# Linear attention and a mixture of adapters on one core: batch 0 loaded in another way, transposes copied in pairs, and a new written-out order

## The chip, the cores and the metric

The kernel runs on one core of a Trainium2 chip. Five engines work side by side, each with its own instruction queue: TensorE (PE in the profile) multiplies matrices and transposes, VectorE (DVE) and ScalarE (ACT) do elementwise work and copy results out of PSUM, GpSimd (POOL) issues the loads, and SyncE (SP) issues the stores. The metric is the device time of one execution in microseconds.

## The reference, cut to what matters

There are 8 batches of 8 heads, 576 positions and 64 features per head, all in float32. Queries and keys go through a relu and are then doubled: once multiplied by the cosine and once by the sine of an angle that grows with the position. The attention is linear, so it is two matrix products and a division:

```
phi(x)  = [relu(x) * cos, relu(x) * sin]       # 128 features
kv      = phi(k)^T v         z = sum over positions of phi(k)
x       = (phi(q) kv) / (phi(q) . z + 1e-6)
```

The heads of a position are put side by side: x has 4608 rows of 512. For every row `logits = x @ w_gate` picks the two largest of 8 experts and weights w from a softmax over the two. The output is `x + sum over the two of w * (x @ A[e]) @ B[e]`, with A of 512x16 and B of 16x512 for each expert.

## The kernel before, in words

**Tiling.** The 4608 rows are worked through in 36 groups of 128 rows. A group is either "one" (two sets of 64 rows of the same batch, position slots x and x+4) or "two" (slot j of two neighbouring batches). The batches form four pairs; the first three pairs have eight groups "one" and one "two" (slot 8), the last pair has nine groups "two". Three groups form a set for the adapters; the last two sets have two groups and one. Sets 0 to 6 cover the first 21 groups.

**Stages of a batch.** K is loaded and gets a relu; V is loaded and multiplied by the cosine and the sine (`vscale`, one call for each); `kv_mm` forms the products K'V in PSUM, and `kv_evac` copies them to the tile BD. Loads by POOL's queue convert float32 to bfloat16 on the way. For batch 0, K and V are loaded by SP's queue as float32 into buffers that later hold outputs (`load_early`). Batches 0 and 1 are loaded in two halves of four heads.

**Stages of a group.** `qt_mm` transposes Q in eight pieces, `qt_evac` copies it to SBUF with a relu (cosine half; the cosine itself cancels in the division), `qt_tan` multiplies by the tangent (the second half), `num_mm` forms numerator and denominator, `x_rden` and `x_xt` divide. `xt_mm` and `xt_evac` transpose x for the adapters.

**Stages of a set.** `za_mm` multiplies by A and the gate weights; eight small steps pick the experts and their weights; `zg_mm` transposes the weighted result; `dx_mm` adds x (a product with the identity) and the adapter's output in PSUM; `osb` copies 128x512 float32 to an output buffer, and `store` writes it. Groups of equal kind and batch that follow each other are stored together. A group "two" is stored from 128 partitions; a group "one" is stored by two transfers, each from 64 partitions, since its halves go to different rows.

**What sets the order.** All steps are entered in a plan with `pl.add` (engine, duration in microseconds, a due time, what it needs, makes and occupies). They are not scheduled at run time: `ORDER` is the sequence in which they are issued, `CHOICE` picks ScalarE or VectorE where a step has both, `SLOTS` gives the buffer of each use. Each engine therefore works through its own steps in the sequence of `ORDER` and waits in place for what a step needs. `HOLD` makes a store wait until a given load has landed. The durations are those that a search used when it wrote the lists; nothing reads them when the kernel is built.

**Buffers.** PSUM has two tiles of two banks (`pND`, for K'V and numerators) and four of one bank (`pS`, for everything else). There are 7 output buffers of three groups each, so a set from 7 on takes the buffer of an earlier set when all stores of that set have landed.

**Stores before.** SP's sequence begins with both halves of set 0, then parts of sets 2, 1, 1, 1, 3, 4 and 4. Three stores are held by loads: the second by V of batch 4, the fourth by K of batch 5, the thirteenth by Q of batch 7.

**Warm-up.** `pe_warm` issues 26 products of a constant tile into an unused bank before any data is there.

Of the kernel before, what the change touches and what calls it, by code (L numbers as in the profile page):

```python
# [9 lines left out]
FP32 = mybir.dt.float32  # L10
# [10 lines left out]
    24, 13, 25, 3, 18, 30, 14, 19, 31, 0, 1, 15, 5, 32, 16, 4, 22, 2, 6, 17, 7, 21, 26, 8, 11, 9, 40, 12, 10, 28, 46,  # L21
    47, 41, 33, 20, 27, 29, 42, 34, 48, 35, 118, 56, 134, 119, 36, 135, 110, 120, 37, 57, 111, 43, 136, 126, 39, 38,
    127, 58, 112, 121, 49, 128, 113, 122, 50, 65, 114, 51, 115, 44, 66, 129, 116, 123, 45, 130, 67, 23, 124, 53, 131,
    117, 74, 132, 125, 137, 138, 133, 52, 139, 75, 142, 55, 54, 398, 143, 150, 399, 140, 151, 144, 166, 400, 403, 145,
    141, 401, 152, 167, 174, 59, 76, 153, 175, 168, 158, 402, 154, 159, 404, 146, 405, 160, 406, 147, 407, 155, 61,
    83, 408, 161, 60, 410, 412, 162, 148, 411, 169, 149, 156, 84, 163, 182, 413, 183, 62, 157, 409, 184, 170, 414,
    176, 164, 171, 64, 190, 416, 191, 85, 68, 63, 177, 192, 165, 185, 178, 417, 172, 186, 421, 418, 179, 419, 187,
    420, 180, 422, 173, 188, 423, 102, 193, 189, 69, 206, 181, 424, 198, 207, 436, 194, 70, 199, 425, 222, 94, 195,
    426, 223, 214, 437, 71, 427, 224, 441, 215, 438, 200, 439, 216, 440, 442, 208, 201, 92, 77, 72, 196, 73, 430, 443,
    428, 197, 431, 209, 202, 203, 429, 444, 230, 210, 445, 204, 231, 217, 79, 101, 78, 446, 450, 415, 447, 448, 205,  # L30
    238, 218, 211, 455, 93, 219, 225, 456, 232, 239, 460, 80, 226, 457, 451, 458, 227, 459, 449, 461, 246, 240, 233,
    81, 462, 452, 254, 247, 234, 463, 262, 235, 82, 103, 434, 278, 263, 248, 241, 86, 279, 249, 433, 255, 464, 212,
    242, 250, 469, 256, 213, 467, 243, 432, 470, 465, 251, 468, 257, 264, 466, 220, 258, 228, 280, 221, 236, 471, 259,
    281, 229, 87, 244, 237, 473, 245, 252, 260, 282, 474, 265, 253, 261, 475, 478, 493, 266, 476, 267, 477, 270, 494,
    268, 271, 479, 498, 480, 269, 310, 272, 481, 311, 495, 88, 273, 482, 286, 318, 287, 487, 274, 496, 275, 497, 483,
    488, 288, 89, 484, 499, 283, 319, 489, 105, 276, 91, 302, 294, 90, 106, 295, 289, 277, 485, 303, 290, 512, 296,
    486, 291, 297, 492, 513, 284, 304, 292, 298, 285, 517, 305, 514, 299, 293, 515, 306, 300, 320, 516, 307, 301, 321,
    518, 312, 530, 322, 500, 308, 519, 501, 309, 313, 531, 502, 95, 520, 521, 505, 532, 104, 526, 506, 533, 522, 314,
    535, 534, 315, 527, 524, 536, 523, 323, 107, 525, 537, 529, 97, 538, 108, 507, 316, 539, 324, 317, 508, 542, 325,
    544, 96, 511, 109, 550, 545, 334, 551, 98, 335, 543, 336, 548, 326, 552, 100, 99, 342, 540, 327, 528, 553, 555,  # L40
    337, 554, 541, 328, 503, 556, 338, 343, 557, 547, 329, 504, 344, 546, 558, 374, 330, 559, 350, 331, 509, 358, 351,
    564, 339, 510, 345, 359, 352, 454, 565, 332, 360, 549, 353, 346, 375, 347, 568, 340, 333, 366, 491, 354, 341, 361,
    367, 355, 348, 562, 368, 349, 362, 356, 376, 369, 563, 363, 357, 569, 453, 370, 371, 364, 382, 570, 365, 372, 377,
    571, 383, 373, 572, 490, 574, 586, 573, 384, 575, 435, 378, 390, 576, 560, 472, 391, 587, 577, 379, 385, 578, 591,
    588, 561, 380, 392, 579, 386, 381, 589, 567, 387, 393, 590, 580, 566, 592, 388, 394, 593, 581, 389, 583, 395, 582,
    594, 603, 584, 595, 396, 604, 596, 585, 397, 605, 608, 598, 606, 607, 600, 597, 609, 610, 599, 622, 601, 611, 632,
    612, 623, 617, 602, 624, 627, 618, 625, 613, 626, 614, 619, 628, 620, 629, 616, 615, 630, 631, 621, 633, 635, 634,
    636,
]
CHOICE = [  # L50
    0, 0, 0, 0, 0, 0, 0, 0, 0, 0, 0, 0, 0, 0, 0, 0, 0, 0, 0, 0, 0, 0, 0, 0, 0, 0, 0, 1, 1, 1, 0, 0, 0, 0, 0, 0, 0, 0,
    1, 0, 0, 0, 0, 0, 0, 1, 0, 0, 0, 1, 1, 0, 0, 0, 0, 1, 0, 0, 0, 0, 0, 1, 0, 0, 0, 0, 0, 0, 0, 0, 0, 0, 0, 0, 0, 0,
    0, 0, 1, 0, 0, 0, 0, 0, 0, 0, 0, 0, 0, 0, 0, 0, 0, 0, 0, 0, 0, 0, 0, 0, 1, 0, 0, 0, 0, 0, 0, 0, 0, 0, 0, 0, 0, 0,
    0, 0, 0, 1, 0, 0, 0, 0, 0, 0, 0, 1, 0, 0, 0, 0, 0, 0, 0, 0, 0, 0, 0, 0, 0, 0, 0, 0, 0, 0, 0, 0, 0, 0, 0, 1, 0, 0,
    0, 0, 0, 0, 0, 1, 0, 0, 0, 0, 0, 0, 0, 1, 0, 0, 0, 0, 0, 0, 0, 0, 0, 0, 0, 0, 0, 0, 0, 0, 0, 0, 0, 0, 0, 0, 0, 0,
    0, 0, 0, 0, 0, 0, 0, 1, 0, 0, 0, 0, 0, 0, 0, 1, 0, 0, 0, 0, 0, 0, 0, 0, 0, 0, 0, 0, 0, 0, 0, 0, 0, 0, 0, 0, 0, 0,
    0, 0, 0, 0, 0, 0, 0, 0, 0, 0, 0, 0, 0, 0, 0, 0, 0, 0, 0, 0, 0, 0, 0, 0, 0, 1, 0, 0, 0, 0, 0, 0, 0, 0, 0, 0, 0, 0,
    0, 0, 0, 0, 0, 0, 0, 0, 0, 0, 0, 0, 0, 0, 0, 0, 0, 0, 0, 0, 0, 0, 0, 0, 0, 0, 0, 0, 0, 0, 0, 0, 0, 0, 0, 0, 0, 0,
    0, 0, 0, 0, 0, 0, 0, 0, 0, 0, 0, 0, 0, 0, 0, 0, 0, 0, 0, 0, 0, 0, 0, 0, 0, 0, 0, 0, 0, 0, 0, 0, 0, 0, 0, 0, 0, 1,
    0, 0, 0, 0, 0, 0, 0, 0, 0, 0, 0, 0, 0, 0, 0, 0, 0, 0, 0, 0, 0, 0, 0, 0, 0, 0, 0, 0, 0, 0, 0, 1, 0, 0, 0, 0, 0, 0,  # L60
    0, 0, 0, 0, 0, 0, 0, 0, 0, 0, 0, 0, 0, 0, 0, 0, 0, 0, 0, 0, 0, 0, 0, 0, 0, 0, 0, 0, 0, 0, 0, 1, 0, 1, 0, 0, 0, 0,
    0, 0, 0, 0, 0, 0, 0, 0, 0, 0, 0, 0, 0, 0, 0, 0, 0, 0, 0, 0, 0, 0, 0, 0, 0, 0, 0, 1, 0, 1, 0, 0, 0, 0, 0, 0, 0, 0,
    0, 0, 0, 0, 0, 0, 0, 0, 1, 0, 0, 0, 0, 0, 0, 0, 0, 0, 0, 0, 0, 0, 0, 0, 0, 0, 0, 0, 0, 0, 0, 0, 0, 0, 0, 0, 0, 0,
    0, 0, 0, 0, 0, 0, 0, 0, 0, 0, 0, 0, 0, 0, 1, 0, 0, 0, 0, 0, 0, 0, 0, 0, 0, 0, 0, 0, 0, 0, 0, 0, 0, 0, 0, 0, 0, 0,
    0, 0, 0, 0, 0, 0, 0, 0, 0, 0, 0, 1, 0, 0, 0, 0, 0, 0, 0, 0, 0, 0, 0, 0, 0, 0, 0, 0, 0, 0, 0, 0, 0, 0, 0, 0, 0, 0,
    0, 0, 0, 0, 0, 0, 0, 0, 0, 0, 0, 0, 0, 0, 0, 0, 0, 0, 0, 0, 0, 0, 0, 0, 0, 1, 0, 0, 0, 0, 0, 1, 0, 0, 0, 0, 0, 0,
    0, 0, 0, 0, 0, 0, 0, 0, 0, 0, 0, 0, 1, 0, 0, 0, 0, 0, 0, 0, 0, 0, 0, 0, 0, 0, 0, 0, 0,
]
SLOTS = [
    0, 0, 1, 0, 1, 0, 2, 3, 0, 0, 0, 0, 1, 1, 1, 1, 2, 1, 2, 2, 0, 2, 3, 2, 3, 0, 0, 3, 1, 3, 4, 1, 1, 0, 0, 0, 0, 2,  # L70
    1, 1, 2, 2, 1, 1, 1, 3, 3, 1, 2, 0, 0, 2, 3, 2, 0, 1, 0, 1, 0, 1, 0, 1, 0, 1, 2, 1, 0, 3, 0, 2, 2, 3, 2, 2, 1, 0,
    1, 3, 3, 3, 0, 4, 0, 2, 4, 0, 4, 2, 5, 1, 0, 5, 3, 5, 3, 0, 0, 1, 6, 1, 0, 0, 6, 1, 2, 7, 2, 1, 2, 7, 1, 0, 8, 0,
# [9 lines left out]
]  # L82

HOLD = [
    (415, 75), (434, 83), (528, 103),
]


# [677 lines left out]
```

## Time and profile before

| | |
|---|---|
| time, median of 3 runs | 114.4 us (112.69 to 114.42) |
| profiled execution: its time | 111.68 us |
| profiled execution: its span | 109.6 us |
| granted TensorE clock | 0.98 of full |
| busy: TensorE, VectorE, ScalarE | 91.0, 94.3, 86.1 us |
| DMA moved | 25.29 MB; HBM read 28.85 MB, written 9.44 MB |

The span runs from the first instruction to the last, and the execution's time has 2.1 us around it. The times in the views are those of that one execution, from the span's start. A line such as `77.55 1.25 PE L417 MATMUL pnd<-VV,Kb ... x72` has start, duration, engine, line, operation, result and operands, form, and how many follow each other. [...] `q0` are the loads of POOL's queue, `q1` the transfers of SP's queue; each has packets, MB, and the time of its packets as a share of 16 DMA engines, which can exceed 100% since packets overlap. The line numbers are those of the kernel before.

### The profile page before, as it was taken

What the parts mean: (1) busy time and instruction counts of PE and PEld (TensorE: products, weight loads), DVE (VectorE), ACT (ScalarE), POOL (GpSimd) and SP (SyncE); (2) the same over time, 40 slices, a digit from 0 to 9 for tenths busy, and PEclk for the clock granted to TensorE, in tenths of its full rate; (3) what the DMA queues carried; (4) which work ended last, traced back from release to release, by engine and by line L of the source; (5) the groups of instructions that cost most, each with busy time, mean ns of one, the idle gap of its engine ahead of it and who ended that gap; (6) DMA issues with size and microseconds to landing.
All of it is one profiled execution on the core that took longest, in us unless ns stands there. A gap on an engine that the chain in (4) does not pass through costs nothing.

```text
span 109.6 us, 4027 instructions
## 1 busy us (share of the span) xinstructions
PE 91.0 (83%) x1670; PEld 65.2 (59%) x1670; DVE 94.3 (86%) x269; ACT 86.1 (78%) x192; POOL 22.8 (21%) x39
## 2 busy tenths in 40 slices
PE   2995296398787959989999989899998999999820
PEld 1342285277556846866878976776676678766200
DVE  5996765986999999999999999999996999887720
ACT  7889558996799639889999699867895987498730
POOL 7981754452222112222200000000000000000000
PEclk9999859999999999999999999999999999999998
DMA  2999999999999999999999999999994999998892
GB/s 76 393 305 269 207 206 193 203 207 210 206 210 209 205 278 209 207 209 277 207 209 307 240 277 207 218 217 256 179 254 103 220 234 285 280 197 226 343 377 109
DMA packets 17041, 25.29 MB, mean 231 GB/s; under 512 B 2176, under 2 KB 13568, under 8 KB 17024
## 3 DMA queue, kind: packets, MB, share of 16 engines
q0 software_dynamic: 13008, 13.25, 72.2%
q1 hardware_dynamic: 4016, 11.80, 34.3%
q8 instruction: 13, 0.21, 0.7%
q14 instruction: 4, 0.03, 0.1%
HBM read 28.85 MB, written 9.44 MB: 349 GB/s over the span
## 4 chain that ended last, share of the span: by engine, by line
DVE 44%; PE 28%; DMA 12%; ACT 6%; issue 4%; POOL 2%; SPq 0%; DVEq 0%; POOLq 0%; ACTq 0%
DVE xt L536 13%; DVE VV L406 10%; DMA Qb<-in_q_dram 8%; PE pnd L520 7%; PE pnd L417 6%; DVE qTcs L507 5%; PE ps L490 5%; DMA out_dram<-osb 4%; PE ps L544 3%; PE ps L557 3%; DVE zg L606 3%; ACT qTcs L495 2%; DVE osb L243 2%; DVE rden L531 2%; DVE BD L431 2%
## 5 line engine op out<-in xcount | busy, mean ns | idle before, releaser
L520 PE MATMUL pnd<-BD,qTcs 128*128 128x130 bf16 (+1 forms) x384 | 23.1, 223 | 3.4 <-DVE xt L536 1.5
L495 ACT ACTIVATE qTcs<-ps 128x512 bf16<-128x512 bf16 x36 | 20.9, 597 | 5.4 <-PE ps L490 4.8
L536 DVE TENSOR_TENSOR xt<-pnd,rden 128x512 bf16<-128x512 f32 x36 | 24.2, 683 | 0.2
L520 PEld LDWEIGHTS <-qTcs 128*128 128x128 bf16 (+1 forms) x384 | 18.2, 103 | 7.3 <-issue 5.1
L241 ACT COPY xT<-ps 128x512 bf16<-128x512 bf16 x26 | 14.6, 588 | 4.2 <-PE ps L544 3.9
L241 ACT COPY osb<-ps 128x512 f32<-128x512 f32 (+1 forms) x31 | 16.4, 558 | 1.4 <-DVE osb L243 1.3
L490 PE MATMUL ps<-ident,Qb 128*64 128x128 bf16 x288 | 14.2, 231 | 3.9 <-DMA Qb<-in_q_dram 3.2
L507 DVE TENSOR_TENSOR qTcs<-qTcs,TT 128x512 bf16<-128x512 bf16 x36 | 14.7, 410 | 2.0 <-ACT qTcs L495 1.6
L544 PE MATMUL ps<-ident,xt 128*128 128x128 bf16 x144 | 13.5, 222 | 2.6 <-DVE xt L536 2.2
L406 DVE TENSOR_TENSOR VV<-Vb,TV 128x2304 bf16<-128x2304 bf16 (+1 forms) x12 | 14.8, 1241 | 0.0
L628 PE MATMUL ps<-Ball,zgT 128*128 128x512 bf16 x36 | 13.7, 380 | 1.0 <-ACT zgT L241 1.0
L490 PEld LDWEIGHTS <-Qb 128*64 128x64 bf16 x288 | 9.7, 114 | 7.7 <-DMA Qb<-in_q_dram 3.7
L626 PE MATMUL ps<-xt,ident 128*128 128x512 bf16 x36 | 13.6, 380 | 0.0
L544 PEld LDWEIGHTS <-xt 128*128 128x128 bf16 x144 | 9.7, 115 | 5.3 <-DVE xt L536 3.2
L404 ACT ACTIVATE VV<-Vb,TVf 128x128 bf16<-128x128 bf16 (+1 forms) x36 | 12.7, 444 | 0.0
L417 PE MATMUL pnd<-VV,Kb 64*64 64x130 bf16 x576 | 11.1, 228 | 0.4 <-DVE xt L536 0.4
L417 PEld LDWEIGHTS <-Kb 64*64 64x64 bf16 x576 | 9.6, 112 | 2.3 <-issue 1.2
L557 PE MATMUL ps<-AW,xT 128*128 128x136 bf16 x144 | 10.7, 223 | 0.1
L429 ACT CAST BD<-pnd 64x520 bf16<-64x520 f32 x13 | 7.8, 597 | 3.6 <-DVE BD L431 2.2
L557 PEld LDWEIGHTS <-xT 128*128 128x128 bf16 x144 | 8.8, 98 | 1.7 <-issue 0.6
L292 PE MATMUL ps<-warm 128*128 128x512 bf16 x26 | 7.8, 474 | 2.0 <-DVE warm L286 2.0
L531 DVE RECIPROCAL rden<-pnd 128x8 f32<-128x8 f32 x36 | 7.2, 200 | 1.0 <-PE pnd L520 0.9
(57 smaller groups left out, 108.1 us busy)
## 6 DMA issues: line engine op xcount, KB each, us to landing
out_dram<-osb SPq DMA_DIRECT2D x16, 256.0 KB, 4.0
Kb<-in_k_dram POOLq DMA_DIRECT2D x6, 576.0 KB, 23.2
Vb<-in_v_dram POOLq DMA_DIRECT2D x6, 576.0 KB, 24.1
Qb<-in_q_dram POOLq DMA_DIRECT2D x6, 576.0 KB, 25.1
out_dram<-osb SPq DMA_DIRECT2D x6, 384.0 KB, 5.3
out_dram<-osb SPq DMA_DIRECT2D x2, 768.0 KB, 3.3
osb<-in_k_dram SPq DMA_DIRECT2D x2, 576.0 KB, 5.6
osb<-in_v_dram SPq DMA_DIRECT2D x2, 576.0 KB, 7.0
```

The lines of the kernel that those rows point to most:

```text
L241: nc.scalar.copy(o, i)
L406: nc.vector.tensor_tensor(out=o, in0=i, in1=TV[:, cs].unsqueeze(1).to_broadcast([128, n, J, D]), op=ALU.mult)
L417: nc.tensor.matmul(out=pt[64 * hh:64 * hh + 64, par, a * 2 * W:(a + 1) * 2 * W], lhsT=kt[r, 2 * a + hh, j, :], rhs=vt[r, 2 * a + hh, j, :] ...
L490: nc.tensor.transpose(out=pt[64 * hh:64 * hh + 64, a, :, x], in_=qt[:, c, j, :], identity=ident)
L495: nc.scalar.activation(tQT[S_(uqt)][:, 0].rearrange("p i x s -> p (i x s)"), pB(up)[:, 0:512], AF.Relu)
L507: nc.vector.tensor_tensor(out=v[1], in0=v[0], in1=f4, op=ALU.mult)
L520: nc.tensor.matmul(out=nd[r, a, 0:4 * W].rearrange("p (h e w) -> p h e w", h=2, e=2)[:, :, par], lhsT=s[:, r], rhs=bd[:, par, a, cs].rearr ...
L536: nc.vector.tensor_tensor(out=tXT[S_(uxt)].rearrange("p (a h d) -> p a h d", a=2, h=4), in0=nd_view(und)[:, :, :, 0:D], in1=tRD[S_(urd)].u ...
L544: nc.tensor.transpose(out=pB(up)[:, c * 128:(c + 1) * 128], in_=tXT[S_(uxt)].rearrange("p (x c) -> p c x", c=4)[:, c], identity=ident)
L557: nc.tensor.matmul(out=pF(uza)[:, n * AW_W:(n + 1) * AW_W], lhsT=tXTT[S_(u)][:, c, :], rhs=AW[:, c, :], start=(c == 0), stop=(c == 3))
L626: nc.tensor.matmul(out=pF(udx), lhsT=ident, rhs=tXT[S_(uxt)], start=True, stop=False)
L628: nc.tensor.matmul(out=pF(udx), lhsT=tZGT[S_(uzt)][:, i], rhs=Ball, start=False, stop=True)
```

## The change

1. **Tables.** The tangents were computed for all positions on every partition (two iotas, two sines, a reciprocal and a product). Now `c_tan_p` computes them from the cosine and sine of nine positions per partition, `c_tan_d` spreads them on the diagonals of a 64x576 float32 tile, and two float32 products with a tile of ones (`c_tan_mm`) copy them to all partitions; ScalarE moves the result to TT.
2. **Warm-up and unused products.** 18 products before the tangents and 18 behind them, in place of 26. `pe_more` adds products that nobody reads: 6 after each K'V product of batches 0 and 1 (four of them), 4 after each of the first five numerators. They write columns of the same PSUM tile that nothing uses.
3. **Batch 0.** Only K stays on SP's queue as float32. V goes with POOL's queue. Q of batch 0 comes in four pieces by position slot (0-1, 4-5, 2-3, 6-8), each with all heads; a group's transposes need only the pieces that hold their slots (`q_needs`).
4. **Pairs.** Two groups in a row share a PSUM bank for their Q transposes, and one copy and one tangent product serve both (20 in place of 36). The same holds for x^T, in the sizes of `XSET` (21 copies in place of 36). The buffers qTcs are 5 of double size (were 8), xT 4 of double size (were 6).
5. **Lists.** `ORDER`, `CHOICE`, `SLOTS` and `HOLD` are new. ScalarE and VectorE now have: x^T copies 18 and 3 (were 26 and 10), output copies 33 and 6 (31 and 8), V scalings 4 and 16 (6 and 14), K relus 4 and 6 (2 and 8), BD copies 12 and 4 (13 and 3). POOL's sequence begins with Q slots 6-8, V first half, the gate weights, Q slots 2-3, Q slots 4-5, V second half, then Q of batch 1 (first half), Q slots 0-1 and the rest of batch 1; A comes after batch 1, B between V and Q of batch 4. The last load is K of batch 7. SP's sequence of stores begins with parts of sets 4, 4, 4, 5, 4, 5, 5, 0, 2, 1, 6, 6, 2, 7, 7, 3, 7, 0, and only the fifth store is held: by K of batch 7.

```diff
 HOLD = [
-    (415, 75), (434, 83), (528, 103),
+    (447, 105),
 ]
...
+    XSET = [2] * 13 + [1, 2, 1, 2, 1, 1, 1, 1]
...
-             "QT": 8, "XT": 16, "XTT": 6,
+             "QT": 5, "XT": 16, "XTT": 4,
...
-    def c_rec():
-        nc.vector.reciprocal(Tsc[:, 0], Tsc[:, 0])
-
-    def c_tan():
-        nc.vector.tensor_tensor(out=TT, in0=Tsc[:, 0], in1=Tsc[:, 1], op=ALU.mult)
+    def c_tan_p():
+        nc.vector.memset(ones_f, 1.0)
+        nc.vector.reciprocal(tan_p, TVf[:, 0])
+        nc.vector.tensor_tensor(out=tan_p, in0=tan_p, in1=TVf[:, 1], op=ALU.mult)
...
+    def c_tan_mm(i):
+        def f():
+            lo, hi = TCUT[i]
+            nc.tensor.matmul(out=pF(("pS", "t", i))[:, 0:hi - lo], lhsT=ones_f,
+                             rhs=tan_d.rearrange("p j s -> p (j s)")[:, lo:hi], start=True, stop=True)
+        return f
...
+    def pe_more(t, n):
+        for _ in range(n):
+            nc.tensor.matmul(out=t[:, 0, 4 * W:512], lhsT=warm[:, 0:128], rhs=warm[:, 4 * W:512], start=True, stop=True,
+                             skip_group_check=True)
...
-    pl.add("warm", one("PE", 7.0, pe_warm(26, ("pS", "w", 0))), -98, needs=["warm"], uses=[("pS", "w", 0)], ins=52)
+    pl.add("warm", one("PE", 5.8, pe_warm(18, ("pS", "w", 0))), -98, needs=["warm"], uses=[("pS", "w", 0)], ins=36)
+    pl.add("warm", one("PE", 3.9, pe_warm(18, ("pS", "w", 1))), -79, needs=[("tan_m", 1)], uses=[("pS", "w", 1)], ins=36)
...
+    QCUT = ((0, 2), (4, 6), (2, 4), (6, 9))
+
+    def load_q0(lo, hi, u):
+        def f():
+            src = q[0].rearrange("(c e) (p j) d -> (e p) c j d", e=2, j=J)[:, :, lo:hi]
+            return nc.gpsimd.dma_start(out=tQ[S_(u)][:, :, lo:hi].rearrange("p c j d -> p c (j d)"),
+                                       in_=src.rearrange("p c j d -> p c (j d)"))
+        return f
...
-    def qt_evac(up, uqt):
-        def f():
-            nc.scalar.activation(tQT[S_(uqt)][:, 0].rearrange("p i x s -> p (i x s)"), pB(up)[:, 0:512], AF.Relu)
+    def qt_evac(gs, up, uqt):
+        def f():
+            n = 512 * len(gs)
+            nc.scalar.activation(tQT[S_(uqt)][:, 0, 0:n], pB(up)[:, 0:n], AF.Relu)
         return f
...
-    def xt_evac(up, uxtt, eng):
-        def f():
-            copy(eng, tXTT[S_(uxtt)].rearrange("p c s -> p (c s)"), pB(up)[:, 0:512])
+    def xt_evac(m, up, uxtt, eng):
+        def f():
+            copy(eng, tXTT[S_(uxtt)].rearrange("p g c s -> p (g c s)")[:, 0:512 * m], pB(up)[:, 0:512 * m])
         return f
...
-    for n, g in enumerate(seq):
+    qset = cut([2, 2, 2, 2, 1] * 4)
+    xset = cut(XSET)
...
+            more = 4 if at[g] < 5 else 0
+            pl.add("num", one("PE", (0.6 if g[0] == "two" else 0.52) + 0.105 * more, num_mm(n, gs, uqt, und, more)), dd + 1.0,
```

## The prediction

> **What bounds the kernel now.** I read the forty slices first, then the chain that ended last, the waits of the store queue, and the DMA traffic stretch by stretch. The slices of the page:
>
> ```profile
> PE   2995296398787959989999989899998999999820
> DVE  5996765986999999999999999999996999887720
> DMA  2999999999999999999999999999994999998892
> GB/s 76 393 305 269 207 206 193 203 207 210 206 210 209 205 278 209 207 209 277 207 209 307 240 277 207 218 217 256 179 254 103 220 234 285 280 197 226 343 377 109
> ```
>
> A slice is 2.74 us. Up to slice 13 (about 35 us) TensorE has holes; from there to 77 us VectorE is full and TensorE nearly so, and from 77 to 96 us the chain is TensorE alone. The DMA engines are busy throughout: at a steady 207 GB/s of loads up to 80 us, then with stores. The end of the chain:
>
> ```profile
> 97.55 0.47 SPq L645
> 98.06 3.95 DMA out_dram<-osb
> 102.06 0.40 DVE osb L243
> ...
> 105.50 0.43 DVE osb L243
> 105.96 0.37 ACT osb L241
> ```
>
> Near the end an output copy waits 3.95 us for a store to free its buffer: stores already touch the path. TensorE around the last load, in the timeline of its matmuls:
>
> ```profile
> 77.55 1.25 PE L417 MATMUL pnd<-VV,Kb 64*64 64x130 bf16 x72 [0.17 <-DVE xt L536]
> 81.63 0.41 PE L490 MATMUL ps<-ident,Qb 128*64 128x128 bf16 x8
> 81.97 1.24 PE L417 MATMUL pnd<-VV,Kb 64*64 64x130 bf16 x72
> ```
>
> The last Q was issued at 54.1 us and landed 27.0 us later, at 81.1; its first transpose runs at 81.63. So loads, TensorE and VectorE all press on the same stretch. The traffic of three stretches, one after another: 84 to 97.5, 97.9 to 100.5 and 101.5 to 103 us:
>
> ```profile
> q1 hardware_dynamic: 1185, 3.28, 96.1%
> DMA packets 147, 0.52 MB, mean 200 GB/s; under 512 B 31, under 2 KB 31, under 8 KB 146
> DMA packets 105, 0.64 MB, mean 426 GB/s; under 512 B 1, under 2 KB 1, under 8 KB 105
> ```
>
> In the middle stretch only two stores of single-batch groups are under way ("half stores", 64 partitions each); in the last a store of 128 partitions ("full"). A half store moves 200 GB/s, a full one 426. In the first stretch the queue is 96.1% busy with 3.28 MB, of which two full stores are 0.52 MB (1.2 us at 426); the rest is 2.76 MB in 12.3 us: **225 GB/s for half stores in a row**.
>
> [...] At 97.5 and 98.1 us the trace has one store of each half together, at 200 GB/s[...] here the granted clock is 0.76 from 13.1 to 20 us, after 3.2 us of waiting.[...]
>
> **The change, part by part.** TensorE pieces of the chain price its work: Q transposes of a group 0.34, numerator products 0.60, x transposes 0.33, za 0.27, zg transposes 0.07, the two output products 0.50, K'V of a batch 1.20 us. Over 36 groups and 8 batches that is 85.6 units in both kernels. Before, 58.3 units precede the K'V at 77.55 us and 63.0 the one at 81.97: time is units plus 19.
>
> *Tables.* Gone are a reciprocal (3.70 us), a product (0.76), two sines (0.68, 0.76) and 0.75 us of iotas. New are four tiny VectorE instructions and one over 64x512 fp32[...], two fp32 products and two ScalarE copies (0.6, 0.2). The products lie between two rounds of warm-up: 18 now start at 1.45 (memset first) and last 6.0 us at the 0.427 and 0.213 us pitch of the trace;[...] 18 more at 0.213 end at 12.4. Before, TensorE's real work began at 13.1 and cold. VectorE sat idle from 9.9 to 11.6, so its 3.5 us saved here end nothing sooner; TensorE gains 0.7 us and 1.5 us of slow clock (16 transposes in 1.07 where 0.68 is normal, two K'V halves at 1.1 and 1.0 for 0.62, eight transposes at 0.57 for 0.34).
>
> *Early loads.* V of batch 0 leaves SP's queue (1.18 MB of fp32) for POOL's, and Q of batch 0 goes in four pieces of 512 packets each. Large casting packets pass at 190 per us over 16 engines (84 ns each); the 800 small ones of A at 18 to 20 us cost 15 ns. Linear in bytes, the pieces cost 23 to 32 ns, 3.3 us for all against 2.7. Bounds: 2.2 us, and 10.8 if every packet costs 84 ns. In the new POOL order the estimated landings are: V halves of batch 0 at 8.6 and 11.5, the last Q piece 13.6, K and V of batch 1 from 15 to 20.4, batch 2 complete at 30, and 15 more loads at 2.85 us (207 GB/s, no stores in between) plus B: the last one, K of batch 7, at **74 us** against 81.1. Every load is issued eight ahead, so POOL's own order isn't late.
>
> *Unused products.* 24 behind the K'V halves of batches 0 and 1 and 20 behind the first five numerators, at 252/512 of 0.213 us: 44 x 0.105 = 4.6 us. TensorE's idle time from 13.1 to 30 us is 4.1 us; they run where it would wait. If those gaps close by themselves, up to 4.6 us come on top; if the clock would fall without them, they gain what it costs. I take nil.
>
> *First 35 us in order.* K'V of batch 0 ends at 16.3 (its V scaling on ScalarE, 2.7 us from 11.5, then Q's transposes), its copies at 17.6, the first numerator at 17.7 (18.23 before). Batch 1 waits for its V and another 2.7 us of ScalarE: numerators from 27.1 (27.2 before), but its transposes are done by then. Batch 2's copies end at 35.6 with 18.0 units done; before, 16.3 at 35.75. I take a **lead of 1.8 us**.
>
> *Pairs.* 16 of 20 Q copies and products hold two groups[...]. With the x copies (10 to 3 on VectorE), three output copies fewer, three large relus that go to ScalarE, one more BD copy and one more V scaling, VectorE loses 4.6 us of work after the start. TensorE is next there and its work is unchanged: worth 0 to 2 us, taken in the lead. A pair holds one of the four banks longer; the price lies between 0 and 1 us.
>
> *Order of the stores.* SP takes its stores in a fixed order, and this is where I put the end. Before, 2.36 MB were stored by 79.5 us and 7.08 MB after. Now the first store belongs to set 4: its output copies stand behind 55.8 units (55.8 + 19 - 1.8 = 73 us), the fourth behind 60.5, the fifth is held until K of batch 7 lands, and the sixth stands behind 62.2: **79.6 us** with its copy (62.2 + 19.2 - 1.8). Sets 0 to 3, finished at 33 to 46 units, are queued behind it. So 5 stores (1.05 MB) are gone, 8.39 MB are left: 5.51 MB half stores at 225 GB/s = 24.5 us, two full ones 1.2 us, the last four 2.36 MB at 426 = 5.5 us. No later store waits for data: the eleventh, at 67.1 units (84.5), comes up at 86. Data end at 79.6 + 31.2 = 110.8; from the last bytes (about 108) to the end of the span the kernel before needs 1.6. **Span 112.4**, +2.8 on 109.6. The profiled execution took 111.68 (2.1 around the span): 114.5 for it. The median of the runs, 114.4, lies 2.7 above that execution; with the same addition I forecast **117.2**.
>
> **Rivals.** *TensorE sets the end* (20%): with the lead of 1.8, TensorE ends at 103.7 instead of 105.5, plus the 4.1 from there to the span's end: 107.8, hence 112.6 us, not slower. It decides if half stores exceed 280 GB/s (5.51 MB in 19.7 us). For it: 92 to 94 us moved 293 GB/s, but with a full store inside; against it every pure stretch, 200 to 238. *The pieces of Q cost full packets* (8%): loads 7.4 us later, K of batch 7 at 81.4, the sixth store at 84.8: 122.4 us. *The start goes wrong* (7%): VectorE stands at batch 1's relu, ahead of the first x, until K lands at 17.7 to 19; another 2 us there, or a clock that falls in spite of the products, gives no lead, the gate 81.5 and 119.1.
>
> **How the numbers follow.** The first case has 65%. Its bounds: half stores at 200 (+3.0) or 265 GB/s (-3.7), the gate at 77.3 (TensorE never idle) or 81.5. A measurement tells about 2% from no change: 112.1 to 116.7. The first case gives 42 slower and 23 within, the two bad starts 15 slower, the TensorE case 10 and 10 (its time lies at the limit): faster 10%, within 33%, slower 57%. The range reaches from the TensorE case to the first with its slow rate, 112.5 to 120.5.
>
> **What would show it.** Right: no store issued before 70 us, the sixth at 78 to 82; loads done by 76; q1 busy without a gap from 80 to the end at 200 to 250 GB/s while half stores run; TensorE done several us before the span. Start: first numerator at about 17.7, clock at 1.0 from 12. Wrong: half stores above 280 GB/s, or TensorE busy to within 4 us of the end.

## The result, and the profile after

The kernel after takes **120.3 us** (median of 4 runs, 119.11 to 120.78), the kernel before 114.14 beside it: **1.0603 times the time** (95% interval 1.0432 to 1.0774), 6.2 us more. The profiled execution took 120.78 us, its span is 118.8 us. The forecast of 117.2 us had the direction and the place; the rise is more than twice the 2.8 us that it gave. Some executions of every kernel here run at a lower granted clock and take longer; ratios and spans below compare the faster ones, medians in microseconds are over all.

The forty slices of the page, each now 2.97 us (TensorE, VectorE, the DMA engines, and their traffic):

```profile
PE   5999978796995596999799989999999999470000
DVE  6924238788899999899998999989998987451000
DMA  3999999999999999999999999018799879989990
GB/s 102 337 165 189 199 208 199 199 207 208 207 209 209 207 207 209 206 210 206 207 208 207 209 212 173 16 44 229 197 276 214 240 199 235 209 274 271 396 398 18
```

Loads run at 207 GB/s with nothing beside them; their packets thin out from 74 us on, and the last one passes at 75.1. Then the DMA engines stand nearly still for two slices (16 and 44 GB/s), and from slice 27 to the end they do nothing but store: ten slices at 197 to 276 GB/s, two at 397. TensorE has nothing left in the last four slices, VectorE in the last three (slices count from 0). The stores of SP's queue (start, duration of the issues, how many; L701 are half stores, L698 full ones):

```profile
76.51 3.98 SPq L701 DMA_DIRECT2D out_dram<-osb  x3
81.70 0.37 SPq L698 DMA_DIRECT2D out_dram<-osb  x1
82.11 8.55 SPq L701 DMA_DIRECT2D out_dram<-osb  x8
90.71 1.20 SPq L698 DMA_DIRECT2D out_dram<-osb  x1
92.01 9.08 SPq L701 DMA_DIRECT2D out_dram<-osb  x7
101.19 1.06 SPq L698 DMA_DIRECT2D out_dram<-osb  x1
102.30 5.71 SPq L701 DMA_DIRECT2D out_dram<-osb  x6
108.10 4.42 SPq L698 DMA_DIRECT2D out_dram<-osb  x4
```

Four stores go out before 82 us, the fifth at 82.11 and the sixth at 83.53; from there it is one store after another. Pieces from the end of the chain that ended last, where TensorE no longer takes part:

```profile
99.28 1.80 SPq L701
...
102.30 1.04 SPq L701
103.38 0.62 SPq L701
104.05 3.41 DMA out_dram<-osb
```

An output copy near the end waits for a buffer, the buffer for its store, the store for the stores ahead of it in the queue. What set the sixth store, in the timelines of TensorE and ScalarE:

```profile
80.03 1.24 PE L444 MATMUL pnd<-VV,Kb 64*64 64x130 bf16 x72
81.20 0.39 PE L682 MATMUL ps<-xt,ident 128*128 128x512 bf16 x1
81.43 0.38 PE L684 MATMUL ps<-Ball,zgT 128*128 128x512 bf16 x1
...
82.43 0.60 ACT L457 CAST BD<-pnd 64x520 bf16<-64x520 f32 x1 [0.76 <-DVE BD L459]
82.93 0.57 ACT L238 COPY osb<-ps 128x512 f32<-128x512 f32 x1
```

The first line is K'V of batch 7. The product that the sixth store writes was issued at 81.43, but its copy (82.93) stands behind a K'V copy of batch 7, before which ScalarE stood still for 0.76 us. The two products start 0.23 us apart and are recorded with 0.39 and 0.38 us, so recorded times of TensorE overlap.

### The profile page after: what moved, and what is told of

It is laid out like the page before. It is cut to its first block, busy times and chain, and to the rows that moved or that the text cites. A ratio compares the mean times of both kernels' runs of the same rounds, so it can differ in the third digit from the quotient of the medians.

```text
span 118.8 us, 4062 instructions
## 1 busy us (share of the span) xinstructions
PE 95.7 (81%) x1728; PEld 69.0 (58%) x1728; DVE 88.5 (74%) x248; ACT 84.1 (71%) x153; POOL 26.1 (22%) x41
## 4 chain that ended last, share of the span: by engine, by line
PE 43%; DMA 16%; ACT 14%; DVE 9%; SPq 6%; issue 3%; DVEq 0%; POOLq 0%; ACTq 0%
PE pnd L574 12%; DMA Vb<-in_v_dram 7%; DMA Qb<-in_q_dram 6%; PE ps L530 6%; SPq L701 5%; PE pnd L444 5%; PE ps L682 5%; PE ps L600 5%; PE ps L684 4%; PE ps L613 4%; ACT BD L457 4%; DMA out_dram<-osb 3%; ACT VV L431 3%; DVE VV L433 3%; ACT qTcs L536 2%
## 5 line engine op out<-in xcount | busy, mean ns | idle before, releaser
L433 DVE TENSOR_TENSOR VV<-Vb,TV 128x2304 bf16<-128x2304 bf16 (+1 forms) x16 | 18.4, 1161 | 7.9 <-DMA Vb<-in_v_dram 7.9
L238 ACT COPY osb<-ps 128x512 f32<-128x512 f32 (+1 forms) x33 | 17.6, 579 | 5.8 <-DVE osb L240 2.6
L536 ACT ACTIVATE qTcs<-ps 128x1024 bf16<-128x1024 bf16 (+1 forms) x20 | 18.2, 948 | 1.9 <-PE ps L530 1.6
L238 ACT COPY xT<-ps 128x1024 bf16<-128x1024 bf16 (+1 forms) x18 | 16.0, 897 | 1.8 <-PE ps L600 1.7
L600 PE MATMUL ps<-ident,xt 128*128 128x128 bf16 x144 | 12.3, 220 | 1.5 <-DVE xt L591 1.2
L556 DVE TENSOR_TENSOR qTcs<-qTcs,TT 128x1024 bf16<-128x1024 bf16 (+1 forms) x20 | 12.3, 624 | 0.9 <-ACT qTcs L536 0.8
L530 PE MATMUL ps<-ident,Qb 128*64 128x128 bf16 x288 | 11.5, 222 | 1.6 <-DMA Qb<-in_q_dram 1.2
L530 PEld LDWEIGHTS <-Qb 128*64 128x64 bf16 x288 | 8.7, 109 | 5.2 <-issue 2.6
L298 PE MATMUL ps<-warm 128*128 128x512 bf16 x36 | 10.2, 448 | 1.5 <-DVE warm L292 1.5
L444 PEld LDWEIGHTS <-Kb 64*64 64x64 bf16 x576 | 8.7, 106 | 2.6 <-issue 2.0
```

Of the source, the lines that this page charges most:

```text
L238: nc.scalar.copy(o, i)
L433: nc.vector.tensor_tensor(out=o, in0=i, in1=TV[:, cs].unsqueeze(1).to_broadcast([128, n, J, D]), op=ALU.mult)
L444: nc.tensor.matmul(out=pt[64 * hh:64 * hh + 64, par, a * 2 * W:(a + 1) * 2 * W], lhsT=kt[r, 2 * a + hh, j, :], rhs=vt[r, 2 * a + hh, j, :] ...
L530: nc.tensor.transpose(out=pt[64 * hh:64 * hh + 64, n, 2 * a:2 * a + 2, x], in_=qt[:, c, j, :], identity=ident)
L536: nc.scalar.activation(tQT[S_(uqt)][:, 0, 0:n], pB(up)[:, 0:n], AF.Relu)
L600: nc.tensor.transpose(out=pB(up)[:, lo:lo + 128], in_=tXT[S_(uxt)].rearrange("p (x c) -> p c x", c=4)[:, c], identity=ident)
```

## The experiments

All ratios are against the kernel before, run on the same chip.

| kernel | ratio (95% interval) | span |
|---|---|---|
| after | 1.0603 (1.0432 to 1.0774) | 118.8 us |
| after, sets 0 and 1 stored early | 1.0194 (1.0130 to 1.0259) | 112.4 |
| after, sets 0 to 2 stored early | 1.0208 (1.0101 to 1.0315) | 114.0 |
| after, finished sets first | 1.0382 (1.0295 to 1.0468) | 115.5 |
| before, stores held | 1.0296 (1.0194 to 1.0398) | 112.9 and 113.7 |
| after, full width, rows permuted | 0.9938 (0.9893 to 0.9984) | 109.0 to 110.4 |
| after, whole stores | 1.0032 (0.9991 to 1.0073) | 110.2 |
| after, whole stores, sets 0 and 1 early | 1.0023 (0.9986 to 1.0059) | 111.6 |
| before, whole stores | 1.0151 (1.0073 to 1.0229) | 112.5 |
| after, no unused products | 1.0601 (1.0503 to 1.0700) | 115.9 |
| after, Q of batch 0 in halves | 1.0493 (1.0373 to 1.0613) | 117.8 |

### When the stores go out

**Sets 0 and 1 early.** Only the order changes: six half stores (371, 372 and 389 to 392, 1.57 MB) stand right behind the copies that they need.

```diff
-    205, 366, 401,
...
-    261, 483, 372, 481,
...
+    205, 366, 372, 371, 401,
...
+    416, 384, 390, 389, 407,
...
+    222, 388, 392, 391, 229,
```

> The changed kernel with the stores of sets 0 and 1 (1.57 MB) issued as soon as each is copied, the rest of the store sequence and its hold unchanged. Store-tail theory: 1.57 MB at 225 GB/s (7 us) leave the tail, the loads are slowed by about 4 us but had some 5 us to spare before the last K'V product at 80.1 us, so the span falls from 118.8 to 111.5-113 us. TensorE theory (the unused products and the late start decide): the span stays within 1 us of 118.8.

114.35 us and 1.0194: 4.1 of the 6.0 points of loss are gone. So with half stores the time at which they go out carries most of the loss, as the theory had it.

**Sets 0 to 2 early**, 2.36 MB, as much as the kernel before had stored by its last load: the same edit with 409, 410 and 411 as well (the last one full).

> The kernel after; only the order is changed: all stores of sets 0, 1 and 2 (2.36 MB, as much as the kernel before had stored by the last load) stand right behind the last output copy that each needs. Theory (the held stores are the loss): 2.36 MB less behind the sixth store is 10.5 us at 225 GB/s, so the queue no longer sets the end; the loads get 2 to 4 us later, K'V of batch 7 at 81 to 82.5, and TensorE with its 24.5 us of work behind that and 4.1 us of output sets a span of 110 to 111: 112 to 113.5 us, level with the kernel before. Rival (bytes are only exchanged): the stores take their full time from the loads, 11.4 us at 207 GB/s, K'V of batch 7 comes at 86 or later and the time is 116 to 118 us, worse than with sets 0 and 1 alone (114.35).

116.1 us, in the range of the rival, though K'V of batch 7 comes at 84.52, between theory and rival (80.03 in the kernel after). By the ratio, 1.0208, it is no better than with 1.57 MB. The longest waits of TensorE from 60 to 90 us, by what ended them, of this kernel and then of the one with sets 0 and 1 (us in total, times, longest):

```profile
PE ps L530 <- DMA Qb<-in_q_dram: 2.9, 2, 1.9
```

```profile
PE ps L530 <- DMA Qb<-in_q_dram: 1.6, 1, 1.6
```

TensorE stands for Q of batches 6 and 7 (with two sets for Q of batch 7 alone), since early stores push the loads back; in the kernel after it has no such wait there. The last packet of the load queue passes at 75.1 (after), 79.6 (two sets) and 81.3 us (three): 4.5 us later for 1.57 MB and 6.2 for 2.36, or 350 and 380 GB/s. Beside loads, half stores cost about what full ones would (4.5 us, where the whole stores of the same 1.57 MB, below, cost 4.4); it is alone that they cost double (217 to 225 GB/s, where whole stores pass at 409). By an estimate from these numbers, each early megabyte takes 2.6 to 2.9 us from the loads and gives back 4.4 behind them (at 225 GB/s), less what TensorE then waits for loads: a third set bought nothing.

**The gate alone.** Nothing is stored before the loads are done, as in the kernel after, but the eleven finished stores of sets 0 to 3 come first.

```diff
 HOLD = [
-    (447, 105),
+    (371, 105),
 ]
...
+    371, 372, 389, 390, 391, 392, 409, 410, 411, 428, 429,
```

> The kernel after with one change of order: the eleven stores of sets 0 to 3, whose data are ready at 33 to 46 units, come first in SP's sequence, and it is the first of them that K of batch 7 holds back. Nothing is stored before the loads are done, as in the kernel after. Theory (it is the gate of the sixth store that counts: finished sets queued behind unfinished ones): the queue starts at 75 and is full from then on; 6.56 MB in half stores at 225 GB/s are 29.1 us, two full ones 1.2, the last four 5.5, so data end at 110.8 and the span at 113 to 114: 115 to 116 us, 4 to 5 under the kernel after. Rival (later stores wait for their data or for buffers in any order, or the early start only makes the queue run dry later): 118.5 to 120.5 us.

117.77 us, by the ratio 2.2 points under the kernel after, where the theory had 4 to 5. The queue starts at 76.4 without a gap, but the stores of sets 4 to 6 now come later, their buffers with them, and TensorE stops in the middle of its work. Its chain between 89 and 95 us:

```profile
89.30 1.05 SPq L701
...
91.03 3.04 DMA out_dram<-osb
94.15 0.70 DVE osb L240
```

The copy that frees a PSUM bank waited for an output buffer, and TensorE was busy for 1.87 of the 5 us from 90 on. So part of the late gate could be had back, and the rest was lost to buffers that the stores of the later sets would have freed.

**The kernel before with its stores held** until the last load (the first three stores moved, one hold in place of three).

```diff
 HOLD = [
-    (415, 75), (434, 83), (528, 103),
+    (414, 103),
 ]
-    170, 414, 176,
...
-    450, 415, 447,
...
-    81, 462, 452, 254,
...
-    82, 103, 434, 278,
+    82, 103, 414, 415, 452, 434, 278,
```

> The kernel before with its first stores moved behind the last load and held until that load (Q of batch 7) has landed; nothing else changed. Store-tail theory: loads land by 75 instead of 81 us, then 9.44 MB of stores take 35 us: span 110.5 to 114 instead of 109.6. If late stores cost nothing, the earlier loads show: 105 to 109.6.

116.91 us, 2.96% slower by the ratio (1.0194 to 1.0398): the kernel before loses some three of the six points by this alone.

### How wide the stores are

**Full width, rows permuted.** Each pair of half stores becomes one store from 128 partitions at the place of the second. To keep one address step, it writes the rows of a pair of batches in another order, so its output is not that of the reference; the number of bytes is the same.

```diff
-                o = out[b * S:(b + 1) * S].rearrange("(p j) d -> p j d", j=J)[:, x + 4 * half:x + 4 * half + n]
-                return nc.sync.dma_start(out=o, in_=tOSB[S_(uo)][64 * half:64 * half + 64, i:i + n])
+                c, y = b // 2 * 2, x + 4 * (b % 2)
+                o = out[c * S:(c + 2) * S].rearrange("(p j) d -> p j d", j=J)[:, y:y + n]
+                return nc.sync.dma_start(out=o, in_=tOSB[S_(uo)][:, i:i + n])
```

> The changed kernel with each pair of half stores replaced by one store of all 128 partitions at the place of the second of the two; the rows of groups of one batch land permuted within their pair of batches, every row of the output is written once. Store-tail theory (a store of 64 partitions runs at half rate): 5.5 MB take 13 us instead of 25, TensorE's end decides instead, span 108 to 110 us. If the limit were the issue of stores or the memory side, the bytes are the same and the span stays at 116 or more.

112.71 us, ratio 0.9938: not measurably different from the kernel before. The order and the hold of the kernel after cost nothing once the stores are wide.

**One store with a step for the two halves** (sets 0 to 2 early), the rows where they belong.

```diff
+                o = out[b * S:(b + 1) * S].rearrange("(p j) d -> p j d", j=J)[:, 0:8].rearrange("p (h j) d -> h p j d", h=2)
+                return nc.sync.dma_start(out=o[:, :, x:x + n], in_=tOSB[S_(uo)][:, i:i + n])
```

> The kernel after with the stores of sets 0, 1 and 2 early, and with each pair of half stores replaced by one store from all 128 partitions, whose address in HBM has a step for the two halves: it writes the same rows and stands at the place of the second. Theory (half stores cost twice, early ones a double share of the loads' time as well): the queue is never full behind the last load, the loads end no later than with half stores, and TensorE sets the end: span 107 to 109.5, time 109 to 112 us, under the kernel before. Rival (the early half stores ran beside the loads at no cost and the end is TensorE's anyway): the same time as with half stores early, 112 to 113.5 us.

205.77 us, a miss of both theories. The traffic from 120 to 140 us, while such stores are under way:

```profile
DMA packets 334, 1.06 MB, mean 53 GB/s; under 512 B 6, under 2 KB 6, under 8 KB 333
q1 hardware_dynamic: 333, 1.04, 12.9%
```

12.9% is the time of about two of sixteen engines (0.129 x 16 = 2.1), at 53 GB/s. The address in HBM has two steps outside here, one for each half; the next run has the two dimensions the other way round.

**Whole stores**, order and hold of the kernel after. The halves are interleaved on the partitions, so that the address has 64 outer steps and two inner ones; each store stands at the place of the first of its pair. The relu copies of Q write the interleaved order, and ScalarE makes a second tangent table TT2 in it.

```diff
+            if gs[0][0] == "one":
+                o = o.rearrange("p (m s x) -> p m x s", x=2, s=NP)
+                i = i.rearrange("p (m x s) -> p m x s", x=2, s=NP)
+            nc.scalar.activation(o, i, AF.Relu)
...
+                o = out[b * S:(b + 1) * S].rearrange("(p j) d -> p j d", j=J)[:, 0:8].rearrange("p (h j) d -> p h j d", h=2)
+                return nc.sync.dma_start(out=o[:, :, x:x + n], in_=tOSB[S_(uo)][:, i:i + n])
```

> The kernel after, order and hold unchanged, with one store from 128 partitions for each pair of half stores, at the place of the first: the two halves of a group are interleaved on the partitions (row 0 of the first, row 0 of the second, row 1 of the first ...), so that the address in HBM has 64 steps outside and two inside. The relu copies of Q write the interleaved order, and ScalarE makes a second table of tangents in that order (about 0.6 us at the start). Theory (half stores cost twice what their bytes need; it is the number of partitions that counts): some 400 GB/s while the queue is full, TensorE sets the end, time 111.5 to 114 us. Rival (two inner rows per partition pair, or the reordering copies of Q, cost what is gained): above 115 us.

113.1 us: 1.0032, the kernel before. **Wider stores take back 5.7 of the 6.0 points.** (That is no share to be added to the 4.1 of early stores: either edit takes from the same loss.) TensorE and traffic by slices of 2.76 us, and one stretch (90 to 95 us):

```profile
PE   4999998897798459689997999999999999999910
GB/s 63 356 198 181 198 206 207 190 207 209 207 209 208 213 203 207 208 207 210 205 207 210 205 213 203 207 168 5 101 156 138 369 415 407 404 375 226 397 296 171
```

```profile
DMA packets 613, 2.04 MB, mean 409 GB/s; under 512 B 76, under 2 KB 76, under 8 KB 612
```

The flow begins as late (the third store at 82.73, the fourth at 84.56 us), the same stretch of idle DMA stands before it, but the stores pass at 409 GB/s and TensorE works up to the end. A gate as late as this one cost nothing here, where the bytes behind it passed at 409 GB/s instead of 217. Whole stores are also fewer and larger; that it is the width that counts is seen in single stores with few others under way. From issue to landing, 256 KB from 64 partitions take 3.0 us (the sixth store of the kernel after), 512 KB from 128 partitions as long (the store at 84.56 here), and 256 KB from 128 partitions 2.1 to 2.2 us (the last store of the kernel before and of this one).

**Whole stores, sets 0 and 1 early**, and **the kernel before with whole stores**:

> The stores of sets 0 and 1 early, and all stores whole, by interleaved partitions. Theory: the queue is never full at the end and TensorE ends 28.6 us after K'V of batch 7; that comes at 80.5 to 81.5, since the early stores still delay the loads: span 109 to 110.5, time 110.5 to 112.5 us, 1 to 3% under the kernel before. Rival (early whole stores delay the loads by more than they save, as the early half stores of three sets did): K'V of batch 7 at 83 or later and 113.5 us or more.

> The kernel before with whole stores, by interleaved partitions, in its own order (each at the place of the first half; the three holds stay on the first of a pair); VectorE makes the second table of tangents at the start, about 0.8 us. Theory (half stores touched its path in the last 10 us, where an output copy waited 3.95 us for one, and delayed its loads before): 1 to 3 us less than before: 110.5 to 113 us. Rival (TensorE sets its end from 77 us on, and the longer start goes straight to it): 114 to 115 us.

With sets 0 and 1 early the time is 114.19 us beside 113.35, ratio 1.0023: no gain over the whole stores alone, and in the range of the rival, though K'V of batch 7, at 82.07, lies between the two. The last load packet passes at 79.7 instead of 75.4 us, 4.4 us late, as with half stores of the same sets. The kernel before with whole stores gets slower if anything, 1.0151, as its rival had it: K'V of batch 2 comes at 36.59 instead of 34.55, of batch 7 at 85.13 instead of 81.97. With its second table VectorE is busy for 95.5 us in all instead of 94.3; how much of the delay is the table, how much the clock (0.945 in this profile, 0.978 in that of before) or the stores, which stand earlier, is not separated.

### The start, and the lead that was not there

**No unused products** (`more = 0` in both places), first with half stores, then with whole ones, where TensorE sets the end:

```diff
-            more = 6 if b in HALF else 0
+            more = 0
...
-            more = 4 if at[g] < 5 else 0
+            more = 0
```

> The changed kernel without the 44 unused products behind K'V and numerators. Store-tail theory: the span moves by 0 to -2 us, as far as the sixth store's data come earlier. TensorE theory: 44 products of 0.105 us are on the path, -4.6 us, 114.2. If they hold the clock up, the clock falls below 1.0 between 13 and 30 us and the first numerator comes later.

> The kernel after with whole stores (interleaved partitions), and without the 44 unused products behind K'V of batches 0 and 1 and the first five numerators. TensorE sets the end here, so what the products cost or gain early shows in the time. Theory A (they delay the copies of K'V and the transposes behind them by about a microsecond, and the lead with it): K'V of batch 7 comes 66 us after that of batch 0 rather than 68, and the time falls by 1 us against the same kernel with them: 111.7 to 112.6 us. Theory B (they are free, as the prediction had it; what the clock loses without them is what they take): within 0.4 us of 113.1.

119.29 us (1.0601, as the kernel after), and 114.43 us with whole stores: 1.0117 (1.0032 to 1.0201) where the same kernel with the products has 1.0032 (0.9991 to 1.0073). That is above what both theories gave, but the intervals overlap. The granted clock by slices, with the products and without, whole stores in both:

```profile
PEclk9999999999999999999999999999999999999995
```

```profile
PEclk9999999999589995999999999999999999999995
```

Without them K'V of batch 2 comes 11.3 us after the last of batch 1, with them 9.7; over all runs the granted clock is 0.943 to 0.972 without them and 0.968 to 0.997 with them. So it seems that they give back in clock what they take. With half stores no such difference is seen (9.1 and 9.2 us, clocks of 0.926 to 0.949 and 0.929 to 0.950). What the runs show is that the products cost nothing measurable: the prediction's "nil" stands.

**Q of batch 0 in halves**, 1568 packets fewer for the same bytes:

```diff
-            src = q[0].rearrange("(c e) (p j) d -> (e p) c j d", e=2, j=J)[:, :, lo:hi]
-            return nc.gpsimd.dma_start(out=tQ[S_(u)][:, :, lo:hi].rearrange("p c j d -> p c (j d)"),
-                                       in_=src.rearrange("p c j d -> p c (j d)"))
+            at = {6: 0, 2: 2}.get(lo)
+            if at is not None:
+                return nc.gpsimd.dma_start(out=flat(tQ[S_(u)])[:, at:at + 2], in_=half_src(q, 0, at // 2))
```

> The kernel after with Q of batch 0 in two loads of four heads (large packets) in place of four pieces by position slot (2048 small packets): the first half where the first piece stood in POOL's queue, the second where the second piece stood; the places of the other two are empty. The same bytes. Theory (a small packet costs what its bytes cost, some 23 to 32 ns): the loads end within 0.8 us of where they did (74 to 75 us), the first numerator within 1.5 us of 18.9, the time within 1 us of the kernel after. Rival (a small packet costs as much as a large one, 84 ns, so that the pieces cost 10.8 us of queue): the loads end 5 us or more sooner, the gates move with them, and the time falls by 2 us or more.

120.43 us, not measurably different from the kernel after (the intervals overlap), and the last load packet passes at 74.9 us instead of 75.1, where the rival needed 5 us or more. The rival of full-price packets is out.

**Where TensorE lost the lead.** Busy time in 35 to 40, 40 to 45 and 45 to 50 us, of the kernel after and then of the one before (TensorE, weight loads, VectorE, ScalarE, GpSimd; clock; DMA):

```profile
35.00:40.00 5.00, 3.52 (x108) 3.04 (x105) 4.70 (x11) 4.98 (x7) 1.48 (x2) 1.00 1.21 208
40.00:45.00 5.00, 3.56 (x105) 3.08 (x106) 5.00 (x13) 3.06 (x5) 1.90 (x3) 1.00 1.22 206
45.00:50.00 5.00, 4.25 (x87) 3.47 (x87) 4.36 (x17) 3.83 (x6) 1.06 (x2) 1.00 1.21 208
```

```profile
35.00:40.00 5.00, 4.11 (x112) 3.31 (x100) 4.75 (x19) 2.46 (x6) 1.34 (x2) 1.00 1.21 236
40.00:45.00 5.00, 4.76 (x125) 3.69 (x129) 4.96 (x14) 4.37 (x9) 1.11 (x2) 1.00 1.18 219
45.00:50.00 5.00, 4.58 (x74) 3.27 (x65) 4.97 (x14) 4.41 (x10) 1.12 (x2) 1.00 1.21 207
```

11.33 us of work against 13.45, 2.1 us lost, in waits around the K'V of batches 2 and 3. Five kernels tried to take them out. The first, with half stores, moves a V scaling of batch 2 and the relu of K of batch 3 from ScalarE to VectorE (`CHOICE` of 64 and 72 from 1 to 0). The others have whole stores. "Copies first" puts batch 2's K'V copies (68, and 67 now on VectorE) ahead of a copy of x^T, and a V scaling of batch 3 (73) behind the first x; the next is the same without the unused products. "Late scaling" puts off the two V scalings of batch 4 (82 and 83); the last has both orders. Copies first, then late scaling:

```diff
-    159, 309, 373, 173, 88, 74, 310, 68, 67, 164, 374, 73, 167,
+    159, 68, 67, 309, 373, 173, 88, 74, 310, 164, 374, 167,
...
-    375, 166, 362,
+    375, 166, 73, 362,
```

```diff
-    376, 82, 97, 377, 393, 76, 379, 83, 77,
+    376, 97, 377, 393, 76, 379, 77,
...
-    189, 369, 209, 106, 368, 197, 219, 370,
+    189, 82, 369, 209, 106, 368, 197, 219, 83, 370,
```

> The kernel after with two steps moved from ScalarE to VectorE: the cosine scaling of V of batch 2 (3.70 us on ScalarE, about 1.3 on VectorE) and the relu of K of batch 3 (2.1 us on ScalarE, 0.7 on VectorE). Theory (the lead of 1.8 us was lost because the copies of batch 2's K'V stood behind that scaling on ScalarE, at 37.4 instead of 35.6): the copies come at 35.5 to 36.5, K'V of batch 3 moves from 42.3 to 40 to 41, K'V of batch 7 from 80.0 to 78 to 79, the sixth store from 83.5 to 81.5 to 82.5, and the time is 1 to 2 us under the kernel after: 118.3 to 119.3 us. Rival (VectorE is as full there, or a later wait such as the landing of a load takes the lead back): K'V of batch 7 within 0.6 us of 80.0, and the time within 0.8 us of the kernel after, or above it.

> The kernel after with whole stores, unused products kept, and an order that serves the path of batch 2: its two K'V copies stand ahead of a copy of x^T, one on ScalarE and one on VectorE instead of both on ScalarE, and one of the two V scalings of batch 3 on VectorE stands behind the first x of batch 2 rather than ahead of it. Theory A (the lead was lost in the queues of ScalarE and VectorE at batch 2): the first numerator of batch 2 comes 1.5 us sooner, TensorE's waits between 35 and 42 us shrink by 1.5 to 2.5 us, K'V of batch 7 by 1 us or more: 111.5 to 112.4 us. Theory B (VectorE is full to 50 us and what is put off there comes back at batch 3): no more than 0.4 us, 112.7 to 113.5 us.

> Both: whole stores, no unused products, and the order that serves batch 2. Theory A on both counts: 110.5 to 111.7 us, 1.5 to 2.5% under the kernel before. Theory B on both: 112.7 to 113.5 us. If only one of them holds: as that one alone.

> The kernel after with whole stores, and the two V scalings of batch 4 on VectorE (1.35 us each, at 42.4 and 43.7 in the kernel after) put off by five and six of its x and table products, to where TensorE has work queued; K'V of batch 4, which needs them, comes at 56. Theory A (four scalings in a row on VectorE between 37 and 45 us took the lead): TensorE's waits of 0.4 to 0.6 us between 44 and 48 us close, K'V of batch 4 comes 0.8 to 1.5 us sooner after K'V of batch 3 (14.4 with whole stores before this edit), K'V of batch 7 as much, and the time is 112 to 112.6 us. Theory B (what is put off is only moved behind the next wait): K'V of batch 4 no sooner, 113 to 114 us.

> The same with the order that serves batch 2 (copies of its K'V ahead of one of x^T and on two engines, one V scaling of batch 3 behind the first x). Theory A (both edits together take the waits out of the stretch from 37 to 48 us): 111 to 112.3 us, under the kernel before. Theory B: 113 to 115.7 us, as with the copies alone.

None is seen to help. The relief of ScalarE gave no ratio: its four runs took 119.3 to 122.6 us, those of the kernel after 119.1 to 120.8. The others took 115.72 (1.0258), 115.08 (1.0222), 114.43 (1.0185) and 117.61 us (1.0427), where whole stores alone have 1.0032; all four came out above what their rivals gave. What became of the wait with the copies first is seen in TensorE's timeline at batch 2, with whole stores, and then with the copies first (the bracket is the idle time before, and what ended it):

```profile
38.39 1.10 PE L584 MATMUL pnd<-BD,qTcs 128*128 128x130 bf16 x16 [1.45 <-ACT BD L460]
40.69 0.41 PE L610 MATMUL ps<-ident,xt 128*128 128x128 bf16 x4 [1.21 <-DVE xt L601]
```

```profile
38.27 1.10 PE L584 MATMUL pnd<-BD,qTcs 128*128 128x130 bf16 x16 [0.72 <-DVE BD L462]
41.32 0.41 PE L610 MATMUL ps<-ident,xt 128*128 128x128 bf16 x4 [1.95 <-DVE xt L601]
```

0.73 us won at the copies, 0.74 lost at the next x. In the late-scaling kernel VectorE has 2.5 us of slack from 40 to 45 and TensorE is no sooner; at 57.2 it then waits 1.64 us for an x behind the scalings. In the profiles of the other four the granted clock also fell, to 0.62 to 0.93 over 5 us between 40 and 50 us, and K'V of batch 3 took 2.17 us instead of 1.24. But the clock also fell there in the profiles of two kernels that have the order of the kernel after up to that point and the same two waits near 38 and 41 us: to 0.66 from 40 to 45 us with Q in halves, and to the digits 5 and 8 (tenths of full) in the slices from 40.4 to 43.3 and 43.3 to 46.2 us with finished sets first. So how much of what the four lost is their order, and how much the clock, is not separated. These runs give no sign that the unused products, or one queue of ScalarE or VectorE alone, took the lead; that it is the sequence of short dependences at a change of batch, with nothing queued on TensorE to fill them, is argued from the waits. Which order would keep the lead stays open.

## Why the prediction was right and wrong

**What held.** No store before 70 us (first at 76.51), loads done by 76 (the last packet at 75.1), half stores at 200 to 250 GB/s (217, below), TensorE done well before the end (last product at 106.6 of 118.8 us). The store queue behind the loads sets the end, and half stores are why: the runs with whole stores show both. That unused products come out at nil, and small packets of Q at the price of their bytes, held. The rival in which TensorE sets the end needed over 280 GB/s from half stores; whole stores give that (409), and the time was then 113.1 us, near the 112.6 that this rival had. That is luck in part, since its span was 107.8 us and the run's is 110.2.

**What failed** is the size of three terms of the sum, and one addition that hid half of it. The sum for the span was 79.6 + 31.2 + 1.6 = 112.4; the trace has 83.5 + 32.7 + 2.6 = 118.8.

- *"I take a lead of 1.8 us"*, and with it the gate at 79.6: **+3.9 us**. K'V of batch 7 came at 80.03, where 1.8 us of lead would have put it at 77.6: 2.4 us. The lead was argued from what VectorE and ScalarE save in all and from the start. The start gave less (the price of the two float32 products of the tables was an estimate that no view of the kernel before showed: they took 1.22 us, from 7.49 to 8.71, and the transposes of Q began at 12.70 instead of 12.4; landings of batch 0 some 1.7 us later than estimated, the first numerator at 18.89 instead of 17.7, the first of batch 1 at 28.8 instead of 27.1), and the waits between 35 and 50 us took the rest. What was saved is also less than argued: VectorE is busy for 5.8 us less in all (88.5 for 94.3), where the prediction's parts add to 8.1. In that sum the saving of a pair was an estimate too, which no view was shown for. Back to back, a tangent product of one group took 0.33 us before (from 45.59 to 45.92), and one of two groups takes 0.60 (51.93 to 52.53): 0.06 us saved by each pair, 1.0 over the 16. The other 1.5 us is "with its copy": the copy of the sixth store's product was priced at 0.2 us behind its place in the units, and stood in ScalarE's queue behind a K'V copy.
- *Half stores at 225 GB/s*: **+1.5 us** for the 31.2. From 83.5 to 107 us 5.36 MB passed; less two full stores (0.52 MB, 1.2 us) that is 4.84 MB in 22.3 us, 217 GB/s, or 0.9 us more for the 5.51 MB. The rest is 0.17 MB of the stores before the sixth, which were still under way: 8.56 MB passed after 83.5, where the sum has 8.39. The 3.2 MB after 107 us, mostly full stores, passed in 9.2.
- *The tail of 1.6 us*, taken from the kernel before: 2.6, **+1.0 us**. The last stores were issued while others were queued, and the very last landed 6.1 us after its issue at 111.35. The last 50 KB of all trickled out from 116.0 to 117.2 us; from the last packet to the end of the span it is 1.6 us again.
- *"With the same addition"*: the median of before lay 2.7 us above its profiled execution, that of after lies 0.5 below. Against the profiled execution the miss is 6.3 us (114.5 forecast, 120.78), against the median 3.1. One profile of a kernel with 2% of scatter was read as typical of its lower end for after as well.

That the range held the time is luck: its top, 120.5, took half stores at 200 GB/s and this addition, while the bound of the gate, 81.5, was too low by 2 us.

## What to carry to other kernels

Here the half stores that waited for the loads to end passed at 217 to 225 GB/s and whole ones at 409, while among the loads the same 1.57 MB delayed the last load packet by 4.5 us as half stores and by 4.4 as whole ones. In a kernel that looks like this one, either widen such stores, or put some of them among the loads, and set against the gain what the compute engines then wait for loads. A lead claimed from an engine's total saving is not a lead: follow the first item of each new batch through every queue in between, and count zero until that path is shorter.

## What the runs showed of the hardware

- Whole stores whose address in HBM has two steps outside passed at 53 GB/s (120 to 140 us, sets 0 to 2 early); those with 64 steps outside and two inside, their halves interleaved on the partitions, at 409 GB/s (90 to 95 us).
- Half stores with no loads beside them passed at 217 to 225 GB/s, whole ones at 409. Among the loads, 1.57 MB of half stores, and 2.36 MB with one full store, delayed the last load packet by 4.5 and 6.2 us (350 and 380 GB/s), and whole stores of 1.57 MB by 4.4.
- In the kernel after, an issue on SP took 0.37 to 0.60 us from 79.4 to 84.6 us, with few stores under way, and 1.0 to 1.8 us five times in a row where they were backed up (96.8 to 103.3 us).
- After two waits of TensorE of 1.24 and 1.17 us that ended near 38.5 and 40.8 us, the granted clock stayed at 1.00 from 40 to 45 us in the profile of the kernel after, and 0.66 in that of Q in halves, which has the same waits (1.24 and 1.17 us). With finished sets first, after waits of 1.23 and 1.17 us, the slices from 40.4 to 43.3 and 43.3 to 46.2 us have the clock digits 5 and 8 (tenths of full).
